# An attention block and two feed-forward layers on one core: earlier loads for the first batch, own buffers for two head pairs, and the next batch's keys ahead of this batch's queries

## The chip, the cores and the metric

The kernel runs on one core of a Trainium2 chip. A core has TensorE (PE in the profile, its weight loads PEld), VectorE (DVE), ScalarE (ACT), GpSimd (POOL) and SyncE (SP, which here issues nearly all DMAs), and 16 DMA engines. The metric is device time in microseconds, from the first to the last instruction, as a median of runs; lower is better.

## The reference

Four batches of eight heads, 576 positions of 64 numbers each, go through a kernelised attention: `phi(x)` projects onto 128 features, subtracts half the squared norm and the row's largest value, and takes the exponential. Then `kv = phi(k)^T v`, `z = sum phi(k)`, and the output of a row is `phi(q) kv / (phi(q) z + 1e-6)`. The 2304 rows of 512 numbers then pass two layers:

```python
h = x @ w_in                       # 512 -> 2048
g = h * (1.0 / (1.0 + np.exp(-1.702 * h)))
x = g @ w_out                      # 2048 -> 512
a = x @ w_a; b = x @ w_b           # 512 -> 1536 each
out = (a * b) @ w_out2             # 1536 -> 512
```

## The kernel before

Every large product is done in f16 with each operand split in a high and a low part, three products in place of one (lines 547 to 549, 575 to 577, 678 to 680, 729 to 731). Weights arrive as 64-bit numbers in chunks of 1 MB (`w_load`, line 182); VectorE puts the bits of a chunk together in three instructions (lines 200, 229, 237), ScalarE writes the high part (247) and VectorE the low part (207). `run` (line 830) takes one such step after each step of the feed-forward generator.

The attention of a batch goes by four head pairs, first four `kphase32`, then four `qphase`. Both begin with `features` (line 335): ScalarE makes the f16 high part of the raw rows (338), VectorE the low part (339), a DMA transposes both (344), ScalarE squares the rows (355, or for the second batch 350, nine pieces with a running sum), TensorE projects (417, 418), VectorE takes the largest values and the biases (402, 408), ScalarE the exponentials (369). A k phase ends with 9 f32 products for `kv` (435, 437) and its copy (442). A q phase of the first two batches transposes the exponentials on TensorE (460), copies them (462), multiplies by `kv` (467), normalises on VectorE (491 to 496), splits the result (522, 523; the 64 rows left over go to `x16r`, 524 and 525) and lets a DMA transpose it into `xT` (529). `xT` has four parts, one for each head pair; each feed-forward product over 512 sums over all four, and TensorE takes its matmuls in order. The later batches do the q side in f16.

The feed-forward pass of a batch (`ffn1`, line 539) has 16 units of hidden columns: 12 matmuls (547 to 549), a tanh and three more steps on ScalarE and VectorE, and 12 matmuls into four accumulators (575 to 577).

What sets the order: the phases are generators. `begin` puts one on a list with the turn at which it starts, `side_step` advances every started one by a step, and each turn is one such round. The first batch's phases are all run through before `ffn1(0)` begins; then, for b = 1 to 3, the k and q phases of batch b are started together with `ffn1(b - 1)`, one turn for each of its 32 steps and the rest of them behind it (`finish_side`, lines 904 and 839). After that the framework's scheduler orders the instructions of each engine. 200 `fillers` (line 874), matmuls of 256 columns whose result nobody reads, are given to it behind the first batch's attention, and it puts them where it takes TensorE to be idle.

Buffers: raw k rows have 3 buffers, raw q rows 4; everything else in `features` and the phases has two (the pool `att`, `bufs=2`), so the third head pair waits for the first to leave its f16 rows (tag A, read by the transpose of line 344) and the fourth for the second. All loads of k, q and v go out on SP's queue; q's first rows are asked for while the last k phase runs, the others one phase ahead of their use, and the next batch's k and v rows behind the last q phase's transpose (lines 853 to 861).

## Time and profile before

| | |
|---|---|
| time, median of 3 runs | 941.8 us (940.66 to 942.13) |
| profiled execution | 940.94 us, span 939.2 us |
| TensorE, weight loads | 902.0 us (96%), 594.6 us |
| VectorE, ScalarE, GpSimd | 559.5 us (60%), 416.1 us (44%), 1.4 us |
| mean granted TensorE clock | 0.998 |
| DMA | 83.91 MB, 89 GB/s over the span |

The busy time of TensorE counts a matmul from its start to a modelled end, so rows of one kind overlap: what one matmul of a dense stretch costs is read from the distance of starts. Until 65.3 us TensorE has only the first batch's attention and the fillers to do (the opening); from 65.3 us on it has the feed-forward passes, with the attention of the following batch between them until about 396 us, and from about 560 us the second layer alone.

### The profile page before, as it was taken

The page shows a single profiled execution, that of the slowest core. Times are in us where ns is not written, and L with a number is a line of the kernel's source. Part 1 is how long each engine was busy: PE and PEld are TensorE (multiplying, and loading weights), DVE is VectorE, ACT ScalarE, POOL GpSimd, SP SyncE. Part 2 cuts the span into 40 slices and gives each one's busy share as a digit, 9 for nine tenths or more (in the row PEclk, how much of TensorE's full clock was granted, in tenths as well). Part 3 has the DMA queues.
Part 4 walks back from the last instruction along what each step waited for, and adds up shares of the span by engine and source line. Part 5 has one row for each costly group of instructions (what it writes and reads, how often), then busy time and mean ns, then how long its engine had stood idle before and what let it go on. Part 6 is the DMA issues. An engine that isn't in the chain of part 4 may idle for free.

```text
span 939.2 us, 16177 instructions
## 1 busy us (share of the span) xinstructions
PE 902.0 (96%) x6666; PEld 594.6 (63%) x6666; DVE 559.5 (60%) x991; ACT 416.1 (44%) x987; POOL 1.4 (0%) x10
## 2 busy tenths in 40 slices
PE   5999999979999999999999999999999999999996
PEld 5884565635554565544448786777776777777683
DVE  5789998488679767698225997263324334222331
ACT  5767776566646465464234452233223222312231
POOL 0000000000000000000000000000000000000000
PEclk9999999999999999999999999999999999999999
DMA  8987569353696424464010431011001000100011
GB/s 188 227 215 219 176 201 265 88 107 83 137 162 164 136 38 79 86 196 135 1 38 8 152 141 46 1 45 46 1 1 35 34 1 1 45 1 1 1 46 23
DMA packets 128457, 83.91 MB, mean 89 GB/s; under 512 B 100480, under 2 KB 109696, under 8 KB 127872
## 3 DMA queue, kind: packets, MB, share of 16 engines
q1 hardware_dynamic: 128384, 82.89, 33.8%
q8 instruction: 52, 0.85, 0.4%
q14 instruction: 21, 0.17, 0.1%
HBM read 54.56 MB, written 9.44 MB: 68 GB/s over the span
## 4 chain that ended last, share of the span: by engine, by line
PE 68%; DVE 14%; ACT 7%; DMA 6%; issue 2%; SPq 1%; ACTq 0%; DVEq 0%
PE o L731 5%; PE o L730 5%; PE o L729 5%; PE ph L547 4%; PE y L576 4%; PE y L577 4%; PE ph L549 4%; PE ph L548 4%; PE y L575 3%; PE pa L437 2%; PE paA L678 2%; PE pbA L678 2%; PE paA L680 2%; PE pbA L680 2%; PE pbA L679 2%
## 5 line engine op out<-in xcount | busy, mean ns | idle before, releaser
L576 PE MATMUL y<-gl,w_out 128*128 128x512 f16 (+1 forms) x320 | 113.5, 358 | 1.0 <-DVE gl L562 0.9
L577 PE MATMUL y<-gh,w_out 128*128 128x512 f16 (+1 forms) x320 | 113.6, 358 | 0.0
L575 PE MATMUL y<-gh,w_out 128*128 128x512 f16 (+1 forms) x320 | 108.4, 358 | 2.4 <-ACT gh L561 2.2
L547 PE MATMUL ph<-xT,w_in 128*128 128x512 f16 x256 | 97.1, 379 | 4.3 <-DMA xT<-x_q_3x 3.7
L548 PE MATMUL ph<-xT,w_in 128*128 128x512 f16 x256 | 97.0, 379 | 0.0
L549 PE MATMUL ph<-xT,w_in 128*128 128x512 f16 x256 | 96.9, 379 | 0.0
L729 PE MATMUL o<-w_o,ab 128*128 128x512 f16 x216 | 82.6, 382 | 1.6 <-ACT ab L710 1.6
L555 DVE SCALAR_TENSOR_TENSOR th<-th,ph 128x512 f32<-128x512 f32 (+1 forms) x80 | 50.3, 630 | 54.7 <-ACT th L552 54.6
L731 PE MATMUL o<-w_o,ab 128*128 128x512 f16 x216 | 82.5, 383 | 0.3 <-DVE ab L711 0.2
L730 PE MATMUL o<-w_o,ab 128*128 128x512 f16 x216 | 82.4, 381 | 0.0
L552 ACT ACTIVATE th<-ph 128x512 f32<-128x512 f32 (+1 forms) x80 | 44.3, 554 | 73.1 <-PE ph L549 68.6
L561 ACT ACTIVATE gh<-th 128x512 f16<-128x512 f32 (+1 forms) x80 | 47.0, 587 | 48.0 <-DVE th L555 47.7
L678 PE MATMUL pbA<-forms,w_b 128*128 128x256 f16 (+1 forms) x240 | 61.0, 262 | 1.4 <-DVE cb L694 1.4
L678 PE MATMUL paA<-forms,w_a 128*128 128x256 f16 (+1 forms) x240 | 60.9, 262 | 1.4 <-DVE ca L694 0.9
L680 PE MATMUL pbA<-forms,w_b 128*128 128x256 f16 (+1 forms) x240 | 61.0, 262 | 0.0
L679 PE MATMUL pbA<-forms,w_b 128*128 128x256 f16 (+1 forms) x240 | 61.0, 262 | 0.0
L694 DVE TENSOR_TENSOR cb<-pbC,kb 128x512 f32<-128x512 f32 (+1 forms) x15 | 9.6, 638 | 86.3 <-PE pbC L680 86.3
L680 PE MATMUL paA<-forms,w_a 128*128 128x256 f16 (+1 forms) x240 | 61.0, 262 | 0.0
L679 PE MATMUL paA<-forms,w_a 128*128 128x256 f16 (+1 forms) x240 | 61.0, 262 | 0.0
L562 DVE SCALAR_TENSOR_TENSOR gl<-th,gh 128x512 f16<-128x512 f32 (+1 forms) x80 | 50.6, 633 | 12.7 <-ACT gh L561 12.6
L686 ACT COPY kb<-pbA 128x512 f32<-128x512 f32 (+1 forms) x30 | 16.3, 543 | 94.0 <-PE pbA L680 94.0
L686 ACT COPY ka<-paA 128x512 f32<-128x512 f32 (+1 forms) x30 | 16.3, 542 | 82.7 <-PE paA L680 78.4
(149 smaller groups left out, 2025.7 us busy)
## 6 DMA issues: line engine op xcount, KB each, us to landing
wraw<-in_moe_w_out_dram SPq DMA_DIRECT2D x14, 1024.0 KB
wraw<-in_moe_w_in_dram SPq DMA_DIRECT2D x8, 1024.0 KB
wraw<-in_moe_w_a_dram SPq DMA_DIRECT2D x6, 1024.0 KB
wraw<-in_moe_w_b_dram SPq DMA_DIRECT2D x6, 1024.0 KB
rawk<-in_k_dram SPq DMA_DIRECT2D x16, 256.0 KB
vt<-in_v_dram SPq DMA_DIRECT2D x16, 256.0 KB
rawq<-in_q_dram SPq DMA_DIRECT2D x16, 256.0 KB
yd<-ye SPq DMA_DIRECT2D x16, 256.0 KB
```

The source lines that it names most:

```text
L547: nc.tensor.matmul(ph[:, :n], w[:, 0, c, fs], xh(c), start=(c == 0), stop=False)
L548: nc.tensor.matmul(ph[:, :n], w[:, 0, c, fs], xl(c), start=False, stop=False)
L549: nc.tensor.matmul(ph[:, :n], w[:, 1, c, fs], xh(c), start=False, stop=(c == KC - 1))
L575: nc.tensor.matmul(o, w[:, 0, f % 4, cs], gh[f][:, :n], start=(f == 0), stop=False)
L576: nc.tensor.matmul(o, w[:, 0, f % 4, cs], gl[f][:, :n], start=False, stop=False)
L577: nc.tensor.matmul(o, w[:, 1, f % 4, cs], gh[f][:, :n], start=False, stop=(f == FC1 - 1))
L678: nc.tensor.matmul(o[:, i], wh, xh, start=first, stop=False, skip_group_check=True)
L679: nc.tensor.matmul(o[:, i], wh, xl, start=False, stop=False, skip_group_check=True)
L680: nc.tensor.matmul(o[:, i], wl, xh, start=False, stop=final, skip_group_check=True)
L729: nc.tensor.matmul(o, lh, w[:, 0, f % 4], start=(f == 0), stop=False)
L730: nc.tensor.matmul(o, lh, w[:, 1, f % 4], start=False, stop=False)
L731: nc.tensor.matmul(o, ll, w[:, 0, f % 4], start=False, stop=(f == FC2 - 1))
```

## The change

In the first batch, k rows of head pairs 1 and 3 are loaded from ScalarE's queue; all q rows are asked for right behind v. Head pairs 2 and 3 of the first batch take their tiles from a pool `spare` of their own, whose space the pool `early` (two weight tiles) takes when it is closed. The raw k rows get a fourth buffer; the pool `att` moves to the right side, and the exponentials of the later batches (`e`) have one buffer in place of two. The cast and subtraction into `x16r` move from ScalarE and VectorE to GpSimd. The fillers go from 200 to 80. The order of the phases changes: `run` takes two turns for each step and a head pair starts every 4 turns in place of 2 (the same spacing); the k phases of batch 1 start at turn 16 after the first four, within the opening, the q phases of a batch start 12 or 4 turns into the pass that they share, the k phases of the batch after it at turn 48 of the 64, and `finish_side(b)` waits for the phases of batch b alone.

```diff
-    START_W, LAG, POST_W, AL = 0, 2, 8, 2
-    VT, FILL = 4, 200
-    RAW = {"k": 3, "q": 4}
+    START_W, LAG, POST_W, AL, SIDE, K1 = 0, 2, 8, 4, 2, 16
+    VT, FILL = 4, 80
+    QB, KB = (12, 4, 4), 48
+    RAW = {"k": 4, "q": 4}
...
-                e = pool.tile([P, 4, M], F32, tag="e", name=f"e_{nm}_{gi}", bufs=2)
+                e = pool.tile([P, 4, M], F32, tag="e", name=f"e_{nm}_{gi}", bufs=1)
...
         nc.scalar.copy(x16[:, 0], xm)
-        nc.vector.tensor_tensor(out=x16[:, 1], in0=xm, in1=x16[:, 0], op=ALU.subtract)
-        nc.scalar.copy(x16r[rows, br, 0, hp, :], xr)
         own["last", b] = nc.vector.tensor_tensor(
+            out=x16[:, 1], in0=xm, in1=x16[:, 0], op=ALU.subtract
+        )
+        nc.gpsimd.tensor_copy(out=x16r[rows, br, 0, hp, :], in_=xr)
+        nc.gpsimd.tensor_tensor(
             out=x16r[rows, br, 1, hp, :], in0=xr, in1=x16r[rows, br, 0, hp, :], op=ALU.subtract
         )
...
+            for _ in range(SIDE):
+                side_step()
+
+    def finish_side(b):
+
+        while any(w[-2] == b for w in waiting + live):
             side_step()
...
+    def home(pool, b, hp):
+        return pool if b or hp < 2 else spare
...
-    with tc.tile_pool(name="att", bufs=2) as att:
+    with tc.tile_pool(name="att", bufs=2, side="right") as att:
+        own["pool"] = att
+
         a_load(att, "k", 0, 0)
+        a_load(att, "k", 0, 1, nc.scalar)
         alloc_own(att)
+        a_load(att, "k", 0, 2)
+        a_load(att, "k", 0, 3, nc.scalar)
         prep(att)
         fillers(1)
-        for hp in range(1, NHP):
-            a_load(att, "k", 0, hp)
...
         v_load(0)
-        finish_side()
+        for hp in range(NHP):
+            a_load(att, "q", 0, hp)
+        begin_k(1, att, psp_att, K1, AL, True)
+        finish_side(0)
+        begun.close()
+        late["early"] = ctx.enter_context(tc.tile_pool(name="early", bufs=1))
         fillers(FILL)
         w_steps(POST_W, NW1)
         for b in range(1, B):
             x1 = x_tile(b, zp, "z")
-            begin_k(b, att, psp_att, 0, AL, b == 1)
-            begin_q(b, att, x1, psp_att, NHP * AL, AL, b == 1)
+            begin_q(b, att, x1, psp_att, QB[b - 1], AL, b == 1)
+            if b + 1 < B:
+                begin_k(b + 1, att, psp_att, KB, AL, False)
             last = own["last", b - 1]
             run(ffn1(b - 1, *xparts(xT), SM), 1, (NW1, NW1 + 2, NWE)[b - 1], last.ins if b > 1 else None)
-            finish_side()
+            finish_side(b)
```

The scheduler's order shows what moves. In the names the first number is the batch, the second the head pair, the last a running number; `x16_q0_3x` is the split result of head pair 3, which the DMA transposes into `xT0`.

SP's queue in the opening, from v's rows to the first weight chunk, before:

```order
L328 DMA vt_112<-in_v_dram 128x8x64 x3
L330 DMA vm_113<-in_v_dram 64x4x64 x2
L344 DMA_TRANSPOSE xt_k0_2_193<-x16_k0_2_190 128x9x128
L344 DMA_TRANSPOSE xt_k0_3_245<-x16_k0_3_242 128x9x128
L316 DMA rawq_0_0_266<-in_q_dram 128x2x256
L320 DMA rawq_0_0_266<-in_q_dram 128x1x64
...
L316 DMA rawq_0_3_464<-in_q_dram 128x2x256
L320 DMA rawq_0_3_464<-in_q_dram 128x1x64
L186 DMA wraw0_1017<-in_moe_w_in_dram 128x4x512
L344 DMA_TRANSPOSE xt_q0_0_310<-x16_q0_0_307 128x9x128
L344 DMA_TRANSPOSE xt_q0_1_376<-x16_q0_1_373 128x9x128
```

and now:

```order
L331 DMA vt_115<-in_v_dram 128x8x64 x2
L333 DMA vm_116<-in_v_dram 64x4x64 x2
L319 DMA rawq_0_0_170<-in_q_dram 128x2x256
L323 DMA rawq_0_0_170<-in_q_dram 128x1x64
...
L319 DMA rawq_0_3_179<-in_q_dram 128x2x256
L323 DMA rawq_0_3_179<-in_q_dram 128x1x64
L347 DMA_TRANSPOSE xt_k0_2_205<-x16_k0_2_202 128x9x128
L347 DMA_TRANSPOSE xt_k0_3_257<-x16_k0_3_254 128x9x128
L347 DMA_TRANSPOSE xt_q0_0_319<-x16_q0_0_316 128x9x128
L347 DMA_TRANSPOSE xt_q0_1_382<-x16_q0_1_379 128x9x128
L189 DMA wraw0_985<-in_moe_w_in_dram 128x4x512
```

The q loads stand ahead of the transposes of k's head pairs 2 and 3, which stood ahead of them, and the two k loads that SP issued between v's are gone.

SP's queue at the end of the opening, where the four parts of `xT0` are transposed, before:

```order
L529 DMA_TRANSPOSE xT0_99<-x16_q0_0x_674 128x8x128
L186 DMA wraw2_1026<-in_moe_w_in_dram 128x4x512
L529 DMA_TRANSPOSE xT0_99<-x16_q0_1x_735 128x8x128
L186 DMA wraw3_1034<-in_moe_w_out_dram 128x2x1024
L529 DMA_TRANSPOSE xT0_99<-x16_q0_2x_781 128x8x128
L320 DMA rawq_1_1_1468<-in_q_dram 128x1x64
L529 DMA_TRANSPOSE xT0_99<-x16_q0_3x_811 128x8x128
L316 DMA rawq_1_2_1586<-in_q_dram 128x2x256
L186 DMA wraw4_1115<-in_moe_w_in_dram 128x4x512
L344 DMA_TRANSPOSE xt_k1_0_1064<-x16_k1_0_1061 128x9x128
L344 DMA_TRANSPOSE xt_k1_1_1121<-x16_k1_1_1118 128x9x128
```

and now:

```order
L534 DMA_TRANSPOSE xT0_99<-x16_q0_0x_674 128x8x128
L189 DMA wraw2_994<-in_moe_w_in_dram 128x4x512
L347 DMA_TRANSPOSE xt_k1_0_734<-x16_k1_0_731 128x9x128
L189 DMA wraw3_1002<-in_moe_w_out_dram 128x2x1024
L534 DMA_TRANSPOSE xT0_99<-x16_q0_1x_751 128x8x128
L534 DMA_TRANSPOSE xT0_99<-x16_q0_2x_797 128x8x128
L347 DMA_TRANSPOSE xt_k1_1_854<-x16_k1_1_851 128x9x128
L319 DMA rawq_1_0_1192<-in_q_dram 128x2x256
...
L319 DMA rawq_1_2_1460<-in_q_dram 128x2x256
L189 DMA wraw4_1137<-in_moe_w_in_dram 128x4x512
L534 DMA_TRANSPOSE xT0_99<-x16_q0_3x_871 128x8x128
```

Two transposes of the second batch's k rows, its q loads and the fifth weight chunk now stand ahead of the fourth part of `xT0`; they stood behind it, but for two q loads.

ScalarE at the same place, before:

```order
L369 ACTIVATE e32_q0_3_504<-pa_690,nb_q0_3_2_688 128x128
L524 CAST x16r_95<-xf_q0_1_679 64x128
L462 COPY eT32_q0_3_760<-pa_761 128x512
L462 COPY eT32_q0_3_760<-pa_767 128x512
L462 COPY eT32_q0_3_760<-pa_773 128x128
L247 ACTIVATE w_out0_89<-wf1_1028 128x1024
L522 CAST x16_q0_2x_781<-xf_q0_2_740 128x512
L524 CAST x16r_95<-xf_q0_2_740 64x128
L522 CAST x16_q0_3x_811<-xf_q0_3_786 128x512
L524 CAST x16r_95<-xf_q0_3_786 64x128
L338 ACTIVATE x16_k1_0_1061<-rawk_1_0_530 128x9x64
```

and now:

```order
L353 ACTIVATE rawk_1_0_530,sq_k1_0_736<-rawk_1_0_530 128x64 x9
L525 CAST x16_q0_1x_751<-xf_q0_1_679 128x512
L465 COPY eT32_q0_3_776<-pa_783 128x512
L465 COPY eT32_q0_3_776<-pa_789 128x128
L525 CAST x16_q0_2x_797<-xf_q0_2_756 128x512
L250 ACTIVATE w_out0_89<-wf1_996 128x1024
L341 ACTIVATE x16_k1_1_851<-rawk_1_1_533 128x9x64
L353 ACTIVATE rawk_1_1_533,sq_k1_1_856<-rawk_1_1_533 128x64 x4
L372 ACTIVATE e32_k1_0_730<-pa_809,nb_k1_0_1_833 128x128 x4
L353 ACTIVATE rawk_1_1_533,sq_k1_1_856<-rawk_1_1_533 128x64 x5
L525 CAST x16_q0_3x_871<-xf_q0_3_802 128x512
```

The work of the second batch's first two k phases now stands ahead of the cast of head pair 3 (`x16_q0_3x`), and the casts into `x16r` are gone.

TensorE at the same place (weight loads left out), before, where 49 filler matmuls follow the last product of the attention:

```order
L467 MATMUL pa_787<-kv32_107,eT32_q0_3_760 128x65 x4
L467 MATMUL pa_794<-kv32_107,eT32_q0_3_760 128x65
L467 MATMUL pa_794<-kv32_107,eT32_q0_3_760 64x65 x2
...
L876 MATMUL idle_98<-om_h_93 128x256
...
L547 MATMUL ph0_0_1039<-xT0_99,w_in0_87 128x512
L548 MATMUL ph0_0_1039<-xT0_99,w_in0_87 128x512
L549 MATMUL ph0_0_1039<-xT0_99,w_in0_87 128x512
```

and now:

```order
L470 MATMUL pa_803<-kv32_110,eT32_q0_3_776 128x65 x4
L552 MATMUL ph0_0_1007<-xT0_99,w_in0_87 128x512
L553 MATMUL ph0_0_1007<-xT0_99,w_in0_87 128x512
L554 MATMUL ph0_0_1007<-xT0_99,w_in0_87 128x512
L470 MATMUL pa_819<-kv32_110,eT32_q0_3_776 128x65 x2
L470 MATMUL pa_819<-kv32_110,eT32_q0_3_776 64x65 x2
...
L420 MATMUL pa_809<-om_h_93,xt_k1_0_734 128x128
L421 MATMUL pa_809<-om_l_94,xt_k1_0_734 128x128
...
L440 MATMUL pa_1028<-vt_115,e32_k1_0_730 128x65 x8
L552 MATMUL ph0_0_1007<-xT0_99,w_in0_87 128x512
```

In place of fillers, TensorE now takes, ahead of its first matmul over the fourth part of `xT0` (the last row), the 18 matmuls of two units over the first three parts, 34 projections of the second batch (the last but two rows are the first of them) and one sum for its `kv`.

## Rows read from the trace of the kernel before

**Rows 1.** The page: busy time, share and instructions of TensorE, its weight loads, VectorE, ScalarE and GpSimd, and the mean busy share of the 16 DMA engines in 40 slices of 23.5 us, in tenths.

```profile
PE 902.0 (96%) x6666; PEld 594.6 (63%) x6666; DVE 559.5 (60%) x991; ACT 416.1 (44%) x987; POOL 1.4 (0%) x10
...
DMA  8987569353696424464010431011001000100011
```

**Rows 2.** Busy time by stretch. Columns: the stretch, its length, busy us and instructions of PE, PEld, DVE, ACT and POOL, the granted clock, the DMA share and GB/s. The opening ends at 65.3; 174 to 198 is the change from the first batch's feed-forward pass to the second's.

```profile
0.00:13.00 13.00, 3.36 (x26) 2.81 (x27) 5.23 (x11) 5.42 (x8) 1.38 (x10) 1.00 0.68 161
13.00:33.00 20.00, 18.69 (x195) 17.45 (x192) 13.70 (x35) 13.63 (x45) 0.00 (x0) 1.00 1.07 211
33.00:65.30 32.30, 31.99 (x324) 29.30 (x325) 26.30 (x73) 22.11 (x63) 0.00 (x0) 1.00 0.89 226
65.30:84.00 18.70, 18.40 (x100) 8.74 (x99) 18.52 (x25) 14.61 (x54) 0.00 (x0) 1.00 0.90 264
84.00:174.00 90.00, 87.95 (x554) 49.43 (x553) 79.98 (x137) 62.73 (x226) 0.00 (x0) 1.00 0.65 188
174.00:198.00 24.00, 18.67 (x128) 12.08 (x126) 15.67 (x35) 13.92 (x31) 0.00 (x0) 1.00 0.50 135
198.00:288.00 90.00, 86.41 (x633) 48.22 (x631) 67.88 (x159) 52.92 (x137) 0.00 (x0) 1.00 0.58 111
288.00:396.00 108.00, 106.05 (x735) 57.76 (x733) 80.20 (x179) 62.59 (x153) 0.00 (x0) 1.00 0.47 106
```

**Rows 3.** Timeline of TensorE in the opening: start, length, line, output and inputs, count. Where rows of one kind follow each other, the distance of their starts is what one costs.

```profile
34.87 1.90 PE L437 MATMUL pa<-vt,e_k 128*128 128x65 f32 x16
36.60 0.22 PE L417 MATMUL pa<-om_h,xt_q 128*128 128x128 f16 x1
36.66 0.22 PE L418 MATMUL pa<-om_l,xt_q 128*128 128x128 f16 x1
...
57.64 2.39 PE L467 MATMUL pa<-kv,eT_q 128*128 128x65 f32 x22
59.96 5.52 PE L876 MATMUL idle<-om_h 128*128 128x256 f16 x49
65.32 0.38 PE L547 MATMUL ph<-xT,w_in 128*128 128x512 f16 x1
65.53 0.38 PE L548 MATMUL ph<-xT,w_in 128*128 128x512 f16 x1
```

**Rows 4.** The columns of the second group (PE and PEld alone) for the instructions of line 876, the filler matmuls, in the opening.

```profile
0.00:65.30 65.30, 25.19 (x201) 19.54 (x201) 1.00 0.90 209
```

**Rows 5.** The chain of waits through the opening, in order of time: start, length, what.

```profile
26.17 6.91 DMA xt_q<-x_q
64.36 0.60 DVE x_q_3x L523
64.99 3.10 DMA xT<-x_q_3x
68.14 0.38 PE ph L547
```

**Rows 6.** Who TensorE waited for between 65.3 and 396 us: total us, times, longest.

```profile
PE pa L417 <- ACT e_k L369: 4.1, 6, 0.9
PE ph L547 <- DMA xT<-x_q_3x: 3.7, 2, 3.5
```

**Rows 7.** The chain of waits at the change from the first to the second batch, columns as in the fifth group.

```profile
189.19 3.04 DMA xT<-x_q_3x
192.28 0.38 PE ph L547
```

**Rows 8.** Groups of VectorE's, then ScalarE's instructions in the opening, shapes apart: line, operation, output and inputs, count, busy us, mean ns of one, idle time before them and what ended it.

```profile
L402 DVE TENSOR_REDUCE mx_k<-pa 128x4 f32<-128x512 f32 x8 | 5.5, 686 | 3.5 <-PE pa L418 3.5
L237 DVE SCALAR_TENSOR_TENSOR wf<-wraw,wf 128x1024 int32<-128x1024 int32 x3 | 3.6, 1204 | 0.0
L339 DVE SCALAR_TENSOR_TENSOR x_k<-rawk,x_k 128x576 f16<-128x576 f32 x4 | 3.0, 758 | 3.4 <-ACT x_k L338 3.3
L525 DVE TENSOR_TENSOR x16r<-xf_q,x16r 64x128 f16<-64x128 f32 x4 | 1.1, 275 | 0.0
...
L369 ACT ACTIVATE e_k<-pa,nb_k 128x128 f32<-128x128 f32 x36 | 10.0, 399 | 1.0 <-DVE nb_k L408 1.0
L338 ACT ACTIVATE x_q<-rawq 128x576 f16<-128x576 f32 x4 | 2.8, 688 | 3.1 <-issue 2.8 <-DMA xt_q<-x_q 0.3
L524 ACT CAST x16r<-xf_q 64x128 f16<-64x128 f32 x4 | 1.2, 306 | 0.0
```

**Rows 9.** Timeline of ScalarE: the second batch's squares with a running sum, two of nine 64-column pieces.

```profile
69.47 0.25 ACT L350 ACTIVATE rawk<-rawk 128x64 f32<-128x64 f32 x1
...
69.71 0.24 ACT L350 ACTIVATE rawk<-rawk 128x64 f32<-128x64 f32 x1
```

**Rows 10.** Busy time by stretch, columns as in the second group: two microseconds in which the DMA engines moved a weight chunk.

```profile
56.00:58.00 2.00, 2.00 (x21) 1.90 (x19) 1.97 (x6) 1.48 (x5) 0.00 (x0) 1.00 0.99 378
```

**Rows 11.** Timeline of GpSimd: its one elementwise row over 128 columns.

```profile
1.50 0.29 POOL masks.py:199 TENSOR_SCALAR_AFFINE_SELECT ident<-ident 128x128 f32<-128x128 f32 x1
```

**Rows 12.** Busy time by stretch near the end of the program, columns as in the second group.

```profile
924.70:926.40 1.70, 0.13 (x3) 0.00 (x0) 0.59 (x2) 1.02 (x1) 0.00 (x0) 1.00 0.00 0
927.95:931.36 3.41, 3.41 (x9) 1.21 (x8) 0.00 (x0) 0.00 (x0) 0.00 (x0) 0.50 0.00 0
```

More of the change, by code (lines that the diff above doesn't have):

```diff
@@ L74, in fused_kernel @@
     ydram = ctx.enter_context(tc.tile_pool(name="ydram", bufs=1, space=bass.MemoryType.DRAM))
-    early = ctx.enter_context(tc.tile_pool(name="early", bufs=1))
+    begun = ExitStack()
+    spare = begun.enter_context(tc.tile_pool(name="spare", bufs=2))
     first = ExitStack()
@@ L94, in ab_tile @@
         if (nm, g) not in w_ab:
-            pool = early if g == 0 else late["pool"] if g < NG - 1 else wts
+            pool = late["early"] if g == 0 else late["pool"] if g < NG - 1 else wts
             tag = f"w{nm}{g}" if g < NG - 1 else "wi"
@@ L291, in prep @@
     def prep(pool):
-        om2 = pool.tile([P, 2, D], F32, tag="om2", name="om2")
-        om = pool.tile([P, D], F32, tag="om", name="om")
+        om2 = pool.tile([P, 2, D], F32, tag="om2", name="om2", bufs=1)
+        om = pool.tile([P, D], F32, tag="om", name="om", bufs=1)
         nc.sync.dma_start(out=om, in_=omega)
@@ L307, in fused_kernel, with a_load @@
     PAIRS = [(0,), (1, 2), (1, 2)]
-    def a_load(pool, kind, b, hp):
+    def a_load(pool, kind, b, hp, queue=nc.sync):
         if b >= B or (kind, b, hp) in raws:
@@ L314, in a_load @@
         h0 = 2 * hp
-        t = pool.tile([P, T, D], F32, tag=f"raw{kind}", name=f"raw{kind}_{b}_{hp}", bufs=RAW[kind])
-        nc.sync.dma_start(
+        t = own["pool"].tile([P, T, D], F32, tag=f"raw{kind}", name=f"raw{kind}_{b}_{hp}", bufs=RAW[kind])
+        queue.dma_start(
             out=t[:, 0 : 2 * NT, :].rearrange("p (h t) d -> p h (t d)", h=2),
@@ L319, in a_load @@
         )
-        nc.sync.dma_start(out=t[:, 2 * NT, :], in_=src[b, h0 : h0 + 2, SM:S, :])
+        queue.dma_start(out=t[:, 2 * NT, :], in_=src[b, h0 : h0 + 2, SM:S, :])
         raws[kind, b, hp] = t
@@ L814, in side_step @@
         while waiting and waiting[0][0] <= turn[0]:
-            live.append(waiting.pop(0)[1])
+            live.append(waiting.pop(0)[1:])
         for g in list(live):
-            if next(g, live) is live:
+            if next(g[1], live) is live:
                 live.remove(g)
@@ L825, in none, with begin @@
         pass
-    def begin(t, gen):
-        waiting.append((turn[0] + t, gen))
+    def begin(t, b, gen):
+        waiting.append((turn[0] + t, b, gen))
+        waiting.sort(key=lambda w: w[0])
     def run(gen, wn=0, wmax=0, after=None):
@@ L836, in run @@
                     w_steps(wn, wmax)
+            for _ in range(SIDE):
+                side_step()
+    def finish_side(b):
+        while any(w[-2] == b for w in waiting + live):
             side_step()
-    def finish_side():
-        while waiting or live:
-            side_step()
+    def home(pool, b, hp):
+        return pool if b or hp < 2 else spare
     def begin_k(b, pool, psp, t0, lag, f32):
@@ L847, in nx @@
                     a_load(pool, "q", b, 0)
-            begin(t0 + lag * hp, kphase32(pool, b, hp, psp, nx, f32))
+            begin(t0 + lag * hp, b, kphase32(home(pool, b, hp), b, hp, psp, nx, f32))
     def begin_q(b, pool, xT, psp, t0, lag, f32):
@@ L861, in nx @@
                         v_load(b + 1)
-            begin(t0 + lag * hp, qphase(pool, b, hp, xT, psp, nx, f32))
+            begin(t0 + lag * hp, b, qphase(home(pool, b, hp), b, hp, xT, psp, nx, f32))
     def xparts(xT):
```

2 lines of the change are left out of this document (1 added, 1 removed).

## The prediction

> **What bounds the kernel now.** I read the page first. TensorE is busy 902 of 939.2 us, and the line of DMA slices stands at 7 to 9 in the first four slices and far lower later [rows 1]. So the kernel is bound by TensorE, and its time is the work that TensorE must do plus the time in which it does none of it. The change leaves the work as it is; only the second part can move. I therefore look next at the stretches [rows 2], for idle time, and at the fillers, which count as busy but are no work.
>
> In the opening TensorE is idle 9.64 + 1.31 + 0.31 = 11.3 us. The 49 fillers before its end take 65.32 - 59.96 = 5.36 us, 0.109 each [rows 3], so the 201 [rows 4] take 21.9. That leaves 65.3 - 11.3 - 21.9 = 32 us of work: TensorE does not set the length of the opening. The chain [rows 5] does: q's transpose lands 6.9 us after its issue, and at the end VectorE finishes the last part of `xT` at 64.96 and its transpose lands at 68.1. Nothing there is slack, though: in the opening VectorE works 5.23 + 13.70 + 26.30 = 45.2 us, ScalarE 41.2, and the DMA engines' shares are 0.68, 1.07 and 0.89 [rows 2].
>
> Behind it TensorE is idle 0.30 and 2.05 us in the first pass, 5.33 between the first and the second, then 3.59 and 1.95 [rows 2]. The 5.33 has one owner: a wait of 3.5 us for the last part of `xT` [rows 6], whose transpose takes 3.04 us [rows 7].
>
> **The change part by part.**
>
> *Opening.* I measure it where the changed TensorE starts its matmuls over the fourth part of `xT0`. By the new order it has then done, beyond the first batch's attention, 18 matmuls of 0.21 us, 34 projections of 0.06 and one `kv` sum of 18 records at (36.60 - 34.87) / 16 = 0.108 [rows 3]: 3.8 + 2.0 + 1.9 = 7.7 us. The kernel before has done as much at 65.3 + 7.7 + 0.3 idle = 73.3. When does the changed one get there?
>
> VectorE must finish the fourth part. Ahead of that the order gives it two more low parts (0.76), three more largest values (two of 0.69, one of about 0.28), three small ones of 0.16 and one weight step (1.2), and takes four `x16r` away (0.275) [rows 8]: 1.5 + 1.7 + 0.5 + 1.2 - 1.1 = +3.8, so 49.0 us of work. ScalarE gets two casts, 18 squares of 0.24 [rows 9] and four exponentials (about 0.28 from start to start), less four casts of 0.31: +5.6, so 47. VectorE's 20.1 us of idle time are 7.8 in the first 13 us, 6.3 up to 33 and 6.0 after it. The first stay: the first k rows have to come. The others shrink, since the q rows are there early and head pairs 2 and 3 no longer wait for the buffers of 0 and 1 (ScalarE's 2.8 us before `x_q` [rows 8] are such a wait); that the transposes of k's pairs 2 and 3 now queue behind the q rows takes some of it back. I take half of them, 6.2: 49.0 + 7.8 + 6.2 = 63.0. The transpose needs 3.1 more [rows 5], and a weight chunk stands just ahead of it, which at 378 GB/s takes 2.8 us [rows 10]; I take one of these. **67**, a gain of 73.3 - 67 = 6.3.
>
> The ends: if no wait is left behind the first 13 us and no transfer stands in the way, 49.0 + 7.8 + 3.1 = 60. If the DMA engines set it: they worked 0.90 of 65.3 = 59 us [rows 4], and now have two transposes (under 2.9 each), a weight chunk (2.8) and about a head pair's q and k rows (some 2) more ahead of that part: 69, at a share of 0.96 done at 72. So a gain of 1 to 13.
>
> *Fillers.* 120 fewer are 13.1 us of matmuls, but they filled waits, and count for nothing by themselves; what they kept up is the clock. Between the last product of the attention and 67 us TensorE now works about 8 of 15 us. The only stretch with such gaps is at the end of the program: after 0.13 us of work in 1.70 the granted clock was 0.50 for 3.41 us, the 1.2 GHz level, which costs 1.7 us [rows 12]. I take 1.5, between nothing and the rival below.
>
> *Change of batches.* In the new order the second batch's q phases are through while two units of the first pass are still to come, and about 18 us of matmuls stand between head pair 3's last product and the first use of its part; before, it was a wait of some 5 us. I take all of the 5.33 and a little of the next such change: **-5.5**. Bounds -4 to -7.
>
> *Later passes.* The k phases of the next batch now run in the pass before. TensorE's waits for a product bank that ScalarE still reads (4.1 us in six [rows 6]) move with them and hardly shrink. The single buffer `e` makes ScalarE wait for VectorE's low part twice in a head pair, and the tanh queues behind; ScalarE is busy 52.9 of 90 us there, so that is covered, and if not it is about 1 us each for eight head pairs. -1.5, bounds -4 to +4. In the first pass VectorE is busy 98.5 of 108.7 us and gets the third batch's k work in addition while the pass stays as long: +0.5, bounds -1 to +6.
>
> *Loads from ScalarE's queue* take about 2 us of it while it waits for the first rows: nothing. *GpSimd*: 32 small rows, about 0.3 us each by its only comparable row [rows 11]; the first reader of `x16r` is hundreds of us later, and `xf` has two buffers: nothing on the path. The Trainium skill (GPSIMD Engine Reference, Key points) says that GpSimd shares its SBUF interfaces with VectorE and contends with it; no run here shows that yet. If VectorE stood still during all of it, it would lose 16 x 2 x 0.29 = 9.3 us and save 16 x 0.275 = 4.4, and half of the difference, 2.4 us, would fall where VectorE is full: the sum would be 931.5 in place of 929.
>
> Sum: -6.3 + 1.5 - 5.5 - 1.5 + 0.5 = -11.3, which makes 929.6 of the profiled 940.94. The median of the runs shown is 0.9 higher; and each wait that goes is worth some 0.15 more than the busy rows show, since a row of 0.38 us has the next start 0.21 behind it [rows 3], 1.5 for about ten of them: **929**.
>
> **The rivals.**
>
> *Short opening.* The half of VectorE's waits that I left in goes too, and the fourth part lands at 60: a gain of 13 and not 6, **922**. For it: ScalarE and VectorE have work ready all the time. Against: the DMA shares.
>
> *DMA engines set the opening* at 72: the fourth part stands behind five weight chunks and all of the second batch's k, v rows: **934**. For it: shares around 0.9 to 1.07 before.
>
> *VectorE paces the first pass*, +6, and the later waits grow by 3: **938**. For it: 98.5 of 108.7. Against: it was as full before, with 2.4 us of waits for TensorE.
>
> *The clock falls, and it is slower.* The order has no filler behind q's first projections but three; before, 110 of them stood there, 12 us. If the clock stays at 1.2 GHz from 33 to 67 us, the 32.3 - 0.3 - 12 + 7.7 = 28 us of work there take 56: the opening ends 22 us later, **951**. It decides from about 18 us of work at the lower level on, as 6 us of gaps and the 12 us of gain are used up first. For it: [rows 12]. Against: a slow TensorE has fewer gaps, and this stretch has work for 28 of 34 us. The Trainium skill (TensorE: Matmul & The Clock Gate, Part 1) says that the lower clock is the default and activity releases it; the trace agrees as far as 0.50 followed the gap.
>
> That the change does not do what it says is ruled out by the order, but it may move work about without effect: **941**.
>
> **How the numbers follow.** Forecast (925 to 933) 0.48; short opening 0.18; DMA 0.15; VectorE 0.08; no effect 0.04; clock 0.07. Less than 0.2% either way, 1.9 us, is no difference that a measurement tells. Faster: 0.48 + 0.18 + 0.15 + 0.08 = 0.89; same 0.04; slower 0.07. The range runs from 914, the short opening with the best later bounds, to 939, which leaves out the clock, no effect, and a little at the low end.
>
> **What would show it.** Right: the matmuls over the fourth part of `xT0` begin at 65 to 69 us; no idle time over 1 us between the passes; VectorE as full as before in the first pass; the granted clock down for a record or two between 50 and 70 us. Wrong: that start before 62 or after 71; a clock of 0.50 for ten us or more; TensorE idle over 5 us in the first pass, with VectorE's line behind it.

## The result, and the profile after the change

The change makes the kernel **slower**: 949.29 us, median of 6 (945.92 to 951.62), against 941.73 of the kernel before on the same chip, ratio 1.0088 with a 95% interval of 1.0072 to 1.0104. The forecast was 929, the range 914 to 939. One part of the change does most of the harm: with the early q rows alone taken back, the kernel takes 939.1, slightly faster than before (run 11).

The profiled execution took 949.55, span 947.7 (before 940.94 and 939.2). The page of the changed kernel, busy tenths, granted clock and DMA share in 40 slices:

```profile
PE   4988999999999999999999999999999999999996
PEclk9987999999999999999999999999999999999998
DMA  7999668653764344360001341011000100100011
```

The same eight stretches as in [rows 2], now of the kernel after:

```profile
0.00:13.00 13.00, 0.45 (x1) 0.18 (x1) 3.08 (x7) 5.31 (x8) 1.38 (x10) 1.00 0.57 146
13.00:33.00 20.00, 18.70 (x189) 17.02 (x190) 13.69 (x37) 12.92 (x38) 0.00 (x0) 1.00 0.97 197
33.00:65.30 32.30, 28.14 (x259) 24.47 (x257) 26.19 (x75) 26.07 (x98) 2.13 (x7) 0.95 0.98 241
65.30:84.00 18.70, 13.21 (x58) 8.12 (x57) 12.95 (x20) 11.38 (x49) 2.48 (x2) 0.60 1.02 198
84.00:174.00 90.00, 89.05 (x557) 50.99 (x556) 82.30 (x141) 60.94 (x207) 4.20 (x6) 0.99 0.72 196
174.00:198.00 24.00, 23.11 (x149) 13.09 (x149) 21.98 (x44) 15.62 (x36) 1.70 (x3) 1.00 0.63 153
198.00:288.00 90.00, 85.74 (x600) 46.06 (x598) 69.50 (x155) 55.74 (x131) 2.81 (x8) 0.98 0.60 135
288.00:396.00 108.00, 103.32 (x720) 56.19 (x719) 80.06 (x176) 62.20 (x148) 2.85 (x8) 1.00 0.43 107
```

Three places differ. Up to 84 us TensorE is idle 12.55 + 1.30 + 4.16 + 5.49 = 23.5 us, against 11.6 before, and its clock falls. Between the first and second pass it is idle 0.89 and not 5.33. From 198 to 396 it is idle 4.26 + 4.68 = 8.9, against 5.5.

Idle time alone misleads in the first place, for 120 fillers are gone: idle time and fillers together (201 and 81 of them, 0.109 us each) are 33.5 us up to 84 before and 32.3 now. What is worse there is the clock: up to 90 us it is at 0.50, the 1.2 GHz level, in three stretches, the longest from 74 to 86 us, soon after two microseconds (70 to 72) with 0.07 us of matmuls. Busy time multiplied by what the granted clock lacks of 1 gives 8.6 us of TensorE's time up to 90 us and 1.7 from 198 to 396, an estimate in slices of half a microsecond; before, it is nothing up to 396.

To see where the 8.5 us of the two spans arise I count the work done, as an estimate from the traces: each matmul but the fillers at the distance of starts that its kind has in dense stretches at a granted clock of 1.00 (0.216 us for 512 columns, 0.109 for 256). Both kernels then do 862.6 us of work. The kernel after is 2.5 us of work ahead of the kernel before at 65.3 us, then behind it: 8.5 at 84, 9.1 at 174, 3.4 at 198, 8.5 at 396. So it loses its time between 65 and 90 us and again in the second and third pass, and the change of batches gives 5.7 back.

TensorE's waits in the kernel after, over the whole span (us in total, times, longest):

```profile
PE pt L303 <- DVE om L299: 10.4, 1, 10.4
PE pa L420 <- ACT e_k L372: 5.2, 5, 2.0
PE pa L485 <- DMA eqT_q<-e_q: 4.0, 2, 2.7
...
PE ph L552 <- DMA xT<-x_q_3x: 2.4, 1, 2.4
```

The first is new in size (omega's rows, 4.8 before), and so is the third, 0.3 us before: products that wait for the transpose of their exponentials.

The end of the opening is in the chain of waits (start, length, what), which answers to [rows 5]:

```profile
68.86 0.68 DVE x_q_3x L526
...
69.87 10.21 DMA xT<-x_q_3x
80.11 0.58 PE ph L552
```

The fourth part of `xT0` is ready on VectorE at 69.5 us, and its transpose, 3.10 us before, takes 10.21. SyncE's queue in front of it shows what it shares the DMA engines with (the last row is the transpose of k's pair 2 of the second batch, just behind):

```profile
65.41 0.57 SPq L319 DMA_DIRECT2D rawq<-in_q_dram  x1
...
66.67 0.45 SPq L319 DMA_DIRECT2D rawq<-in_q_dram  x1
...
67.76 0.87 SPq L319 DMA_DIRECT2D rawq<-in_q_dram  x1
68.97 0.37 SPq L189 DMA_DIRECT2D wraw<-in_moe_w_in_dram  x1
69.87 1.27 SPq L534 DMA_TRANSPOSE xT<-x_q_3x  x1
71.25 6.07 SPq L347 DMA_TRANSPOSE xt_k<-x_k  x1
```

The q rows of three head pairs (two issues each, the last one's second comes later) and a chunk of 1 MB were issued in the 4.5 us ahead of it. The Trainium skill (DMA: Bandwidth & Descriptors, Queues, rings and completion order) says that each DMA engine consumes descriptors in ring order, though a later one may finish its write before an earlier one. The traces agree with the order: 3.10 us in the kernel before, with one load of 32 KB in the 2 us ahead, and 10.21 behind 1.8 MB. The size varies: with the same issues ahead it took 6.88 in the profile of run 5.

### The profile page after: what moved, and what is told of

It is laid out like the page before. It is cut to its first block, busy times and chain, and to the rows that moved or that the text cites. A ratio compares the mean times of both kernels' runs of the same rounds, so it can differ in the third digit from the quotient of the medians.

```text
span 947.7 us, 15943 instructions
## 1 busy us (share of the span) xinstructions
PE 900.5 (95%) x6546; PEld 588.5 (62%) x6546; DVE 552.8 (58%) x975; ACT 413.5 (44%) x971; POOL 17.5 (2%) x42
## 4 chain that ended last, share of the span: by engine, by line
PE 66%; DVE 17%; DMA 7%; ACT 6%; issue 2%; SPq 2%; ACTq 0%; DVEq 0%
PE o L736 5%; PE o L734 5%; PE o L735 5%; PE y L581 4%; PE ph L552 4%; PE ph L553 4%; PE y L580 4%; PE y L582 4%; PE ph L554 3%; PE paA L683 2%; PE pbA L683 2%; PE paA L685 2%; PE pbA L685 2%; PE pbA L684 2%; PE paA L684 2%
## 5 line engine op out<-in xcount | busy, mean ns | idle before, releaser
L552 PE MATMUL ph<-xT,w_in 128*128 128x512 f16 x256 | 98.9, 387 | 4.7 <-DMA xT<-x_q_3x 2.4
L553 PE MATMUL ph<-xT,w_in 128*128 128x512 f16 x256 | 99.1, 387 | 0.0
L554 PE MATMUL ph<-xT,w_in 128*128 128x512 f16 x256 | 98.9, 386 | 0.0
```

Of the source, the lines that this page charges most:

```text
L552: nc.tensor.matmul(ph[:, :n], w[:, 0, c, fs], xh(c), start=(c == 0), stop=False)
L553: nc.tensor.matmul(ph[:, :n], w[:, 0, c, fs], xl(c), start=False, stop=False)
L554: nc.tensor.matmul(ph[:, :n], w[:, 1, c, fs], xh(c), start=False, stop=(c == KC - 1))
```

## The experiments

Ratios are against the kernel before on the same chip. Executions of one kernel differ by 3 to 11 us from the fastest to the slowest, so a single profile shows where time went, and the medians how much.

**1. Is it the clock, for lack of fillers?**

```diff
-    VT, FILL = 4, 80
+    VT, FILL = 4, 200
```

> The changed kernel with 200 fillers in place of 80, all else as in the change. Three theories. Transfer: the first pass starts late because the transpose of the fourth part of xT0 took 10.2 us (3.1 before), behind the second batch's k transposes, its q rows and a weight chunk; the half clock is mostly a consequence. Then the matmuls over the fourth part still start at 78 to 80 us, and only the 6 us of work that ran at half clock behind that point (80.1 to 86.1) give back 3, with 1 more from the two short records before: 945 to 946 us. Clock: the missing fillers made the 24 us at 0.50 that the changed kernel shows, and those lengthened the opening; with 200 the clock stays at 1.00 up to the end, the fourth part starts by 72 and the time falls by about 10, to 939. Late start: omega's rows land at 9.9 us and not at 4.4; the fillers change nothing in that: 949.

950.58, ratio 1.0093 (1.0077 to 1.0110): no gain. Its stretches, and the start of the matmuls over the fourth part:

```profile
33.00:65.30 32.30, 32.30 (x334) 30.25 (x333) 26.01 (x74) 25.72 (x95) 2.11 (x6) 1.00 0.95 227
65.30:84.00 18.70, 15.83 (x107) 10.74 (x106) 14.65 (x25) 13.03 (x53) 1.64 (x2) 0.91 0.91 202
```

```profile
75.21 0.38 PE L552 MATMUL ph<-xT,w_in 128*128 128x512 f16 x1 [2.57 <-DMA xT<-x_q_3x]
```

The clock is back for the most part (1.00 and 0.91 in place of 0.95 and 0.60) and the time is not, as only the third theory had it. So more fillers are no remedy. That the clock costs nothing is not shown, for the 120 fillers take 13.1 us of TensorE in exchange, and in run 15 as many cost 7.5. But the fall goes with the waits: run 11 has no more fillers than the change, and its clock is 1.00 from 65 to 84 us. The part also starts 5 us sooner and that is not in the time either: that start alone does not measure the opening, as I had taken it to.

**2. Second batch's k phases behind the opening.**

```diff
-    START_W, LAG, POST_W, AL, SIDE, K1 = 0, 2, 8, 4, 2, 16
+    START_W, LAG, POST_W, AL, SIDE, K1 = 0, 2, 8, 4, 2, 26
```

> The changed kernel with K1 at 26 in place of 16: the second batch's k phases start ten turns later, behind the first batch's last phase; fillers stay at 80. Transfer: the k transposes (three of some 2.9 us) and a weight chunk no longer stand around the fourth part's transpose, which then takes 3 to 4 us; VectorE also finishes the part 1 to 2 us sooner, so the matmuls over it start at 71 to 73 in place of 80.1, and the time falls by 5 to 8, to 941 to 944; some comes back if the first pass now waits for its k work. Clock: with as few fillers and less work in the stretch the clock falls as long as before, and the time stays within 2 us of 949. Late start: the same 949.

950.01, ratio 1.0101 (1.0075 to 1.0126). The place behaves as expected, the time does not: the matmuls over the part start at 70.9, and the later passes give it back (the profile is of an execution of 947.3 us).

```profile
198.00:288.00 90.00, 83.91 (x620) 47.18 (x619) 68.11 (x159) 53.48 (x132) 2.81 (x8) 0.98 0.59 136
288.00:396.00 108.00, 102.47 (x700) 54.94 (x697) 84.22 (x181) 63.96 (x151) 2.85 (x8) 0.98 0.45 107
```

Idle 6.1 + 5.5 there, and not 4.3 + 4.7. By the count of work, this run is 5.5 us ahead of the kernel after at 198 us and 0.7 at 396. What takes it there is not shown.

**3. Late omega; 4. casts back on ScalarE and VectorE.**

```diff
+        prep(att)
         a_load(att, "k", 0, 2)
         a_load(att, "k", 0, 3, nc.scalar)
-        prep(att)
```

> The changed kernel with omega's rows issued behind head pair 0's k rows, ahead of those of head pairs 2 and 3, as the kernel before has it; the order that follows also puts the fourth part's transpose ahead of a weight chunk. Late start: VectorE starts at 4 to 5 us in place of 9.9 and the first transpose 3.9 us sooner, and the whole opening moves by 4 to 5: 944 to 945. Transfer: the engines of the DMA are the bound by the end of the opening, so an earlier start alone is worth under 2, but the chunk that no longer stands ahead of the part gives 2.8: fourth part at 75 to 77, 945 to 947. Clock: as few fillers, so the half clock stays and the time is within 2 us of 949.

946.12, ratio 1.0048 (1.0028 to 1.0068): 3 us, short of what late start said and within what transfer said; the order also put a chunk behind the part's transpose, so the two are not separated here.

```diff
-        nc.gpsimd.tensor_copy(out=x16r[rows, br, 0, hp, :], in_=xr)
-        nc.gpsimd.tensor_tensor(
+        nc.scalar.copy(x16r[rows, br, 0, hp, :], xr)
+        own["last", b] = nc.vector.tensor_tensor(
```

> The changed kernel with the casts of the last rows (x16r) back on ScalarE and VectorE, all else as in the change. If GpSimd's 32 rows (17.5 us of POOL with the sets, up to 1.8 us for two in the opening) hold VectorE up: 2 to 3 us faster, 946 to 947. If they hide: VectorE has four more instructions of 0.275 in the opening and ScalarE four of 0.31, the time within 1.5 us of 949, on either side.

954.26, ratio 1.0130 (1.0101 to 1.0158): 5 slower, outside both. Taking them off GpSimd gains nothing here; what they gain or cost by themselves is not settled, as run 8 says the opposite.

**5 and 7. The later passes: distance of the products, and the single buffer `e`.**

```diff
                 in_=e16.rearrange("p l t m -> p (l t m)"),
             )
             yield
             yield
+            yield
+            yield
```

```diff
-    RAW = {"k": 4, "q": 4}
+    RAW = {"k": 3, "q": 4}
-                e = pool.tile([P, 4, M], F32, tag="e", name=f"e_{nm}_{gi}", bufs=1)
+                e = pool.tile([P, 4, M], F32, tag="e", name=f"e_{nm}_{gi}", bufs=2)
```

> The changed kernel with two more turns between a head pair's transpose of its exponentials (eqT) and the products that read it, batches 2 to 4 only (the change advances each phase two turns per unit of the pass, so that the distance was halved to one unit). Fewer units: the 5 us by which the changed kernel falls behind in its second and third pass (258 to 376 us) are this wait, 4.0 us in two in TensorE's waits and one fall of the clock behind it: they go, and the time falls by 4 to 5, to 945. Single buffer e: the products wait because the exponentials come late, one after the other through one buffer; two turns more hide only part: 948 or no difference. Opening: untouched by this edit, the fourth part of xT0 starts at 80 us as before.

> The changed kernel with two buffers for the exponentials e in place of one; the k rows have three buffers in place of four to make room, as before the change. Single buffer e: the later passes get back their 4 to 5 us, and the long waits for e_k and e_q on TensorE go: 945. Fewer units: the products still stand one unit behind the transpose, so the wait of 2.7 us for eqT stays and the time is within 2 us of 949.

948.39, ratio 1.0065 (1.0040 to 1.0090), within the noise of no change; and 946.62, ratio 1.0051 (1.0037 to 1.0066), a gain of 2.7, between the two theories, and in run 16 the same edit loses time.

**6. K1 at 26, omega first and the two turns together.**

> The changed kernel with three edits together: K1 at 26, omega's rows behind head pair 0's k rows, two more turns ahead of the products. If the losses are the three places named so far (fourth part's transpose behind the second batch's work, 7 us in the profile of the kernel with K1 at 26; late omega 2 to 3; products on the heels of their transpose 4 to 5), they add up: 949 - 7 - 2 - 5 = 935, some 6 us below the kernel before. If the work that K1 moves out of the opening only queues up in the second pass, whatever the distance of the products, 2 to 4 of it stay lost: 938 to 943.

946.84, ratio 1.0039 (1.0024 to 1.0054). They don't add up to 14 us but to 2.5, outside both theories: my list of causes lacked the main one.

**8. The kernel before with the casts on GpSimd alone.**

> The kernel before with one part of the change alone: the casts of the last rows (x16r) on GpSimd. Without them the changed kernel took 5 us longer, which no theory of mine had. If they relieve VectorE and ScalarE where the passes wait for these: 2 to 5 us faster than before, 937 to 940. If that came from the order that the scheduler found in that build and not from the casts: within 1.5 us of 941.7.

944.34, ratio 1.0029 (1.0005 to 1.0053): slightly slower, outside both theories. So the casts on GpSimd cost 2.3 us in one order and save 5 in the other. A new order by the scheduler may make such a difference; that it does here, and a price of their own, is not shown.

**9. Transfers cleared.** Run 6, and the second batch's k and v rows asked for behind the part's transpose:

```diff
-        nc.sync.dma_start_transpose(
+        part = nc.sync.dma_start_transpose(
             out=xT[:, hp].rearrange("p l (t c) -> p (l t) c", t=NT),
...
+        if b == 0 and hp + 1 == NHP:
+            with tc.issue_after(part.ins):
+                for i in range(NHP):
+                    a_load(pool, "k", 1, i)
+                v_load(1)
+                a_load(pool, "q", 1, 0)
```

> The kernel with the three edits together, and in addition the second batch's k and v rows are asked for only behind the transpose of the fourth part of xT0. There that transpose took 7.67 us, from 61.5 to 69.2, though VectorE was done at 61.3. Transfer: it now takes 3 to 4 us, the matmuls over the fourth part start at 64 to 66 us, earlier than in the kernel before (68.1), and if nothing else is late the time falls by 3 to 5 from 946.8, to 943. Moved only: the second batch's k phases now wait for their rows in the first pass, as long as the transpose won: 946 to 950.

949.45, ratio 1.0072 (1.0049 to 1.0096). That is as "moved only" said. The transpose still took 6 us, with a chunk 0.7 us ahead of it, and ScalarE then waited 2.8 us for the k rows:

```profile
61.87 0.37 SPq L189 DMA_DIRECT2D wraw<-in_moe_w_in_dram  x1
62.56 1.23 SPq L536 DMA_TRANSPOSE xT<-x_q_3x  x1
```

```profile
68.61 0.58 PE L560 MATMUL ph<-xT,w_in 128*128 128x512 f16 x1 [5.29 <-DMA xT<-x_q_3x]
```

**10. Opening undone; 12. and the later passes mended** (the edit below, q rows as in run 11, K1 at 26, 200 fillers; 12 adds the edits of 5 and 7).

```diff
-        a_load(att, "k", 0, 1, nc.scalar)
         alloc_own(att)
-        a_load(att, "k", 0, 2)
-        a_load(att, "k", 0, 3, nc.scalar)
         prep(att)
         fillers(1)
+        for hp in range(1, NHP):
+            a_load(att, "k", 0, hp)
```

> The changed kernel with the opening of the kernel before: k rows all from SyncE's queue behind omega, q rows as they are asked for, the second batch's k phases ten turns later (K1 at 26), 200 fillers; the buffers of two head pairs, the casts on GpSimd, the order of later batches and the single buffer e stay. If the opening is what the change lost (some 10 us more of idle time and fillers by the first pass's end) and the change of batches what it gained (some 6), with 5 lost in the passes behind: 939 to 941. If the later work queues up as it did with K1 at 26 alone: 945 or more.

> The kernel with the opening undone, and in addition two turns more between the transpose of the exponentials and their products and two buffers e (three for the k rows): the best version of these parts. If the later losses are these two: 3 to 5 us below the kernel with the opening undone alone, 935 to 938, faster than the kernel before. If GpSimd's casts and the two steps per unit cost time by themselves: 940 to 943.

944.73, ratio 1.0024 (1.0009 to 1.0038), and 954.60, ratio 1.0129 (1.0103 to 1.0155). The first gives back 4.6 of the 7.6 us lost, less than the first theory; by runs 11, 14 and 15 it undoes one part that harms together with parts that help. The second is a clear miss: two edits that had cost nothing (runs 5 and 7) cost 10 here, and why stays open.

**11. Only the early q rows taken back.**

```diff
         v_load(0)
-        for hp in range(NHP):
-            a_load(att, "q", 0, hp)
```

> The changed kernel with one part undone: the q rows of the first batch are asked for as before, not beside v. In the change k's pair 2 is transposed at 22.6 us and not at 15.5, behind the four pairs of q rows in SyncE's queue and in ScalarE's and VectorE's order. If those early q rows lengthen the opening: pair 2's transpose at 18 to 19 (omega stays late), the opening 2 to 4 us shorter, 945 to 947. If they shorten it, as predicted: 2 to 4 us slower, 951 to 953. If the transfers set its end in any case: within 1.5 us of 949.

939.08, ratio 0.9974 (0.9958 to 0.9989): 10.2 us less than the changed kernel, more than any theory had, and 0.3% less than the kernel before. SyncE's queue in the kernel after, the q rows ahead of the transposes of k's pairs 2 and 3:

```profile
16.77 0.60 SPq L319 DMA_DIRECT2D rawq<-in_q_dram  x1
...
21.91 0.54 SPq L323 DMA_DIRECT2D rawq<-in_q_dram  x1
22.55 4.07 SPq L347 DMA_TRANSPOSE xt_k<-x_k  x2
26.72 2.81 SPq L347 DMA_TRANSPOSE xt_q<-x_q  x2
```

and with the q rows back:

```profile
17.10 2.75 SPq L347 DMA_TRANSPOSE xt_k<-x_k  x2
19.90 0.60 SPq L319 DMA_DIRECT2D rawq<-in_q_dram  x1
...
24.57 0.53 SPq L323 DMA_DIRECT2D rawq<-in_q_dram  x1
27.35 1.34 SPq L347 DMA_TRANSPOSE xt_q<-x_q  x1
```

The k transposes go out 5.4 us sooner, and q's first one only 0.6 later. It is the queue that held them, for VectorE had the low parts of all four pairs ready long before, in the kernel after by 12.2 and 15.1 us (0.3 later in this run):

```profile
10.13 2.09 DVE L342 SCALAR_TENSOR_TENSOR x_k<-rawk,x_k 128x576 f16<-128x576 f32 x3
...
14.31 0.75 DVE L342 SCALAR_TENSOR_TENSOR x_k<-rawk,x_k 128x576 f16<-128x576 f32 x1
```

The chain of this run at the end of the opening, and the stretches of the first pass's start and of its later passes:

```profile
66.00 0.68 DVE x_q_3x L526
66.71 6.03 DMA xT<-x_q_3x
72.78 0.38 PE ph L552
```

```profile
65.30:84.00 18.70, 13.88 (x88) 7.67 (x86) 16.01 (x26) 13.03 (x46) 0.00 (x0) 1.00 0.93 240
...
198.00:288.00 90.00, 86.16 (x607) 45.61 (x607) 73.92 (x163) 55.15 (x131) 2.82 (x8) 1.00 0.61 138
288.00:396.00 108.00, 105.30 (x716) 56.62 (x715) 83.80 (x178) 61.70 (x143) 2.86 (x8) 1.00 0.42 105
```

The part is ready 2.9 us sooner, its transpose is 4.2 shorter (ahead of it a chunk and the first q rows of one head pair, not of three), the clock is 1.00 and not 0.60 from 65 to 84 us, and 2.4 of idle time go from the passes behind. By the count of work this run is ahead of the kernel after by 8.2 us at 174, 7.3 at 198, 11.2 at 396. No run moves the two transposes alone with all else in place, so these figures hold what the scheduler made of the rest too.

**13 to 16, on run 11's kernel:** the edit of run 3 (13), the one shown at run 10 (14), 200 fillers (15), and run 13 with the edit of run 7 (16).

> The kernel with the q rows put back, and omega's rows issued behind head pair 0's k rows. The order of SyncE's queue is otherwise nearly the same, so this is the price of the late omega by itself. Late start: VectorE starts at 5 to 7 us and not at 10, k's pair 0 is transposed 2 to 4 us sooner, the opening is 2 to 3 shorter: 936 to 937. Transfers: the DMA engines' share is near 1 up to the fourth part, so the start is worth nothing: within 1 us of 939.

> The kernel with the q rows put back, and all k rows on SyncE's queue behind omega, as in the kernel before: the part of the change that loads from ScalarE's queue is undone. If the second queue is worth something once omega is early: slower than the kernel with omega first, 938 to 940. If its only effect was to delay omega: 936 to 937, as with omega first.

> The kernel with the q rows put back, with 200 fillers in place of 80. The clock was at 0.50 in a record or two there as well. Clock, as the prediction's sum had it: 1.5 to 2 us faster, 937. Fillers of 0.11 us each stand in front of work that has become ready, as they did with 200 in the changed kernel: no difference, 939 to 940.

> The kernel with the q rows put back and omega first, with two buffers e and three for the k rows. In the changed kernel these two buffers gave 2.7 us. If the single e costs that in the later passes: 2 to 3 us below the kernel with omega first. If the 2.7 came from three k buffers in the opening (fewer k rows ahead of the fourth part): no gain here beyond 1 us, since the opening no longer waits for them.

13: 937.96, ratio 0.9952 (0.9938 to 0.9967), the best version with 17 and 18; against run 11 the intervals overlap, so omega's price by itself is not shown, though the first transpose of k goes out at 8.3 and not at 11.2. 14: 943.37, ratio 1.0013 (0.9992 to 1.0034): in this version **ScalarE's queue is worth 5 us**, more than expected (omega is issued at 2.0 us in both). 15: 946.58, ratio 1.0059 (1.0038 to 1.0080), 7.5 slower than with 80, where both theories said no loss. The early q rows themselves can be priced in three versions: 10.2 us in the change, 8.2 with omega first (run 3 against 13), 4.0 with 200 fillers (run 1 against 15). 16: 944.66, ratio 1.0023 (1.0005 to 1.0042), 6.7 slower: in this version the change's single `e` with four k buffers is the better pair.

**17. Next batch's rows behind `eqT`; 18. 40 fillers** (both on run 13's kernel). 17, for batches 3 and 4:

```diff
-            nc.sync.dma_start_transpose(
+            turned = nc.sync.dma_start_transpose(
                 out=eqT.rearrange("p l t m -> p (l t) m"),
...
+            if hp + 1 == NHP:
+                next_rows(pool, b, turned)
```

`next_rows` holds the loads of the next batch's k and v rows, which waited for the last transpose of line 347 before.

> The kernel with the q rows put back and omega first, and one thing more: in batches 3 and 4 the next batch's k and v rows are asked for behind the transpose of head pair 3's exponentials (eqT), not ahead of those of pairs 2 and 3. In the changed kernel these 14 loads held SyncE's queue from 244.9 to 257.7 us, with an eqT behind them that TensorE then waited 2.7 us for. Queue: the waits for eqT (3.2 us in three in the kernel without this edit) go, 2 to 3 us faster, 935 to 936. Transfer time alone: the transposes still take 3 to 5 us and the products still follow one unit behind, so the waits stay, within 1 us of 938.

> The kernel with the q rows put back and omega first, with 40 fillers in place of 80; with 200 in place of 80 (and omega late) it became 7 us slower. If each filler behind the first k pair takes 0.11 us from work that is ready: 1 to 2 us faster, 936 to 937. If the clock then falls in the opening: slower, 939 to 942. If the 7 us came from the other order that the scheduler made of it, further back: within 1 us of 938.

17: 938.56, ratio 0.9970 (0.9957 to 0.9983), no gain, as the second theory said. TensorE's wait from 198 to 396 us in run 13, then in run 17:

```profile
PE pa L485 <- DMA eqT_q<-e_q: 3.2, 3, 1.8
```

```profile
PE pa L495 <- DMA eqT_q<-e_q: 2.9, 3, 1.4
```

The wait is the same with the 14 loads out of the way, so they were not its main cause. 18: 937.42, ratio 0.9953 (0.9939 to 0.9967), as with 80: 40 fillers more or less make no difference that the runs tell. Whether run 15's 7.5 us are the price of its 120 more or of another order of the phases I did not take apart.

## Why the prediction was wrong

**Opening, -6.3.** This is the step that failed. The fourth part's matmuls were to start at 67 and start at 80.1; the 13 us are two terms of similar size, 6.5 each. Two of the signs of being wrong came: this start, and a clock of 0.50 for over ten us.

First, VectorE's waits. I took half of those behind 13 us, on the ground that the q rows come early, and noted that the k transposes behind them take some back. None went: up to 69.54 VectorE is idle 6.31 from 13 to 33 us and 6.1 after it, 12.4, as much as the 12.3 before. The work was less than reckoned (47.2 us, not 49.0), and 9.9 us, not 7.8, are lost in the first 13, because omega lands late: 47.2 + 9.9 + 12.4 = 69.5, not 63.0. The early q rows are one reason: they delay k's transposes by 5.4 us, q's products need the k sums first, and q's own transposes gain 0.6 (run 11). But without them VectorE is still idle 5.9 + 5.0 = 10.9 us behind 13 us, up to 66.68. So half of the waits don't go in either case: VectorE waits for other products in place of those that it waited for, 5.7 us for the projections of k in run 11, against 3.5 before. What holds them up there stays open. I had the two queue orders side by side and read from them that something was earlier; which of the two moved rows was waited for first was the question.

Second, the transpose: 3.1 and one of a chunk's 2.8 us, against 10.2 measured. I left out what else is issued just ahead, the q rows of three head pairs, and k's transpose just behind, and took a third of the chunk. With the chunk ahead and k rows behind it is 6.0 in run 9, near 3.1 + 2.8, and with q rows ahead and the chunk behind 5.59 in run 1. What each adds to the 10.2 is not separated.

That the fourth part's start measures the opening failed as well: it moved by 5 and 9 us in runs 1 and 2 with no effect on the time.

**Fillers and clock, +1.5.** The clock fell further than I took: 8.6 us of TensorE's time up to 90 us, where I had 1.5. How much of that the kernel's time feels is open: 200 fillers bring the clock back and not the time (run 1), and 40 lose more of the clock than 80, 5.0 us against 1.7, and the kernel takes as long (runs 18 and 13). The rival of 951 has nearly the time that came, but not by its mechanism: it had the clock at 1.2 GHz from 33 to 67 us and the opening 22 us longer, and the clock was 0.95 up to 65.3 and fell behind it. Its time was luck.

**Change of batches, -5.5.** Right: 5.33 became 0.89, and the count of work gives 5.7.

**Later passes, -1.5 (bounds -4 to +4).** The second part of the miss: outside my bounds, they cost 5.1 us by the count of work, 3.4 of it idle time and 1.7 the clock. More distance (run 5) gains nothing clear, moving SyncE's loads (17) leaves the waits for `eqT`, and two buffers `e` gain 2.7 in one version (7) and lose 6.7 in another (16). With the early q rows gone 3.9 of the 5.1 go (run 11); how the opening reaches so far, and the rest, stay open.

**VectorE in the first pass, +0.5.** It is as full as I said (82.3 of 90 us) and TensorE idle 0.95: right.

**ScalarE's queue, nothing.** Wrong both ways: the order of loads that came with it issues omega at 4.3 and not at 2.0 us, and in the version with omega first the second queue is worth 5 us (run 14 against 13).

**GpSimd, nothing.** The casts are at my 0.3 us in the middle and the subtractions at 0.42 (below). The 2.4 us that I named for a VectorE that stands still beside them did not come: in the trace its instructions beside them are longer by about 1 us in all, less than the 4.4 us that it no longer works. Runs 4 and 8 disagree on what is left in the time.

**Sum.** The profiles differ by +8.5 us where the sum had -11.3, a miss of 19.8. By the count of work, the opening, the fillers and the first pass were to give 4.3 and lost 9.1, 13.4 of the miss; the change of batches gave 0.2 more than forecast; the later passes make 6.6. With the early q rows gone (run 11) 8.2 of the 13.4 and 3.9 of the 6.6 are found. In the medians: 939.1 without them, 938.0 with omega first, 11 of 20 us. Of the other 9, most lies before 174 us, where VectorE's waits were not halved and the transpose still takes 6.03 us in run 11, and 2.7 in the later passes; their causes stay open.

## What to carry to other kernels

On an in-order queue, an early load is a late something else: list what it passes, and ask which of the two is waited for first. A transpose at the end of a chain shares the engines with what is issued just around it (3.1 us became 5.6 to 10 here), so its own time alone is no price. When work that only fills gaps is taken away, add it to the idle time before two profiles are compared. And where a scheduler orders the work, an edit can be worth something else in every version, even with the other sign (runs 4 and 8, 7 and 16): test a part in the version in which it is to stand.

## What the runs showed of the hardware

GpSimd's casts depend on what else runs. All 32 of the kernel after, beside the 0.29 of [rows 11]: durations in ns, least, median and most:

```profile
L529 POOL CAST x16r<-xf_q x16: 282/287/1288, 49.9 to 376.4; 64x128 f16<-64x128 f32 x16
L530 POOL TENSOR_TENSOR x16r<-xf_q,x16r x16: 418/424/1283, 50.3 to 376.8; 64x128 f16<-64x128 f32 x16
```

A full VectorE alone does not make them long. At 239.60 us a cast keeps its 0.28 us beside an instruction of VectorE that reads a product bank (`pa`); at 65.28 it takes 1.21 beside one that reads `wf`, a tile in SBUF (the memory of the tile pools):

```profile
239.45 0.68 DVE L405 TENSOR_REDUCE mx_q<-pa 128x4 f32<-128x512 f32 x1
239.60 0.28 POOL L529 CAST x16r<-xf_q 64x128 f16<-64x128 f32 x1 [59.40 <-DVE xf_q L499]
...
65.13 1.21 DVE L232 SCALAR_TENSOR_TENSOR wf<-wraw,wf 128x1024 int32<-128x1024 int32 x1
65.28 1.21 POOL L529 CAST x16r<-xf_q 64x128 f16<-64x128 f32 x1 [7.30 <-DVE xf_q L499]
```

Eight of the 32 rows take 0.69 us or more. Each of them starts while VectorE is at a full tile in SBUF (`wf`, `w_out`, `x_q`, `gl`), and ends 0.14 to 0.29 us behind that instruction. VectorE pays less, but it pays: its `x_q` at 141.84 us, which starts in the middle of a subtraction on GpSimd, takes 0.98 in place of 0.75. The Trainium skill (GPSIMD Engine Reference, Key points) says that GpSimd shares its SBUF interfaces with VectorE and contends with those of its instructions that run in a 2-port mode or have two SBUF inputs; the trace agrees as far as the rows beside `pa` stay short.
